# Sliding-window attention with a cosine-gated dense layer on one core: dense slots of two 256-token chunks in 512-column matmuls, a half-angle gate under a checked bound, late attention in two banks

## The chip, the cores and the metric

The kernel runs on one core of one Trainium2 chip. The metric is the device time of one execution in microseconds (us). The kernel before takes 733.99 us, the median of three runs (732.23 to 734.21).

## The reference

q, k and v have the shape (4 batches, 8 heads, 768 positions, 64). Attention keeps the first four positions (the sinks) and a window of 128 before each query. The dense layer has 3072 tokens, a model width of 512 and a hidden width of 2048, and its weights come as fp64.

```python
keep   = (pos[None, :] < n_sink) | ((rel >= 0) & (rel < window))     # rel = pos[:, None] - pos[None, :]
scores = where(keep, q @ k.T / sqrt(64), -1e9)
a      = exp(scores - max);  a = a / (sum(a) + 1e-9)
x      = (a @ v).transpose(0, 2, 1, 3).reshape(3072, 512)
h      = x @ w_in                # 512 -> 2048
g      = h * cos(h)
out    = g @ w_out               # 2048 -> 512
```

## The kernel before, in words

All large products run on PE as three fp32r matmuls, high by high, high by low and low by high, after each operand has been split into a high part (a rounding copy, on ACT) and a low part (a subtraction, on DVE).

The 3072 tokens are 12 chunks of 256 tokens (two query blocks of one batch). A chunk first goes through attention head by head. The heads of three of the four chunks that start a batch (24 heads) are "early": natural loads, turned on PE with transposes (L734), scores and values in plain fp32 matmuls (L771, L989), and the split of the result with a PE matmul that subtracts the high part (L340). The other 72 heads are "late": turned by DVE, split, scores L827 into bank `s`; the probabilities are turned on PE (L937) into bank `tp`, from where L960 (ACT) and L965 (DVE) read them; values L1013 go to bank `av`, read by L1020 (ACT) and L1027 (DVE). The sink columns of four heads at a time are turned on PE (L921), into bank `av` too.

Then the chunk goes through 8 dense slots, 96 slots in all. A slot takes two tiles of 128 hidden columns for the chunk's 256 tokens: 24 matmuls of 256 columns into one PSUM bank h (L391), whole turns of the angle on ACT (L400) and their removal on DVE (L406), the cosine on ACT (L413), the product h times cosine on DVE (L418), the high part of g on ACT (L424) and its low part on DVE or POOL (L430), and 12 matmuls of 512 columns (L439) that add into the chunk's two accumulator banks b0 and b1. Three banks take turns for h from the third chunk on. `xhi` and `xlo`, the split tokens, have two buffers each, so the next chunk's are written while this chunk's are read.

The weights are loaded as raw fp64 in pieces of 512 columns. Four bit operations and one subtraction turn a piece into fp32 and its two parts (L499, L505, L511, L535 on DVE, L532 on ACT). 32 pieces do this in the first sixth of the run, and later a DVE instruction a piece (L550) looks for weights that are too small for this. 120 fill matmuls (L1281), which compute nothing that is used, stand between the first instructions of PE.

The order of the instructions on each engine is fixed when the kernel is built: a planner lists the steps by due times, which the table C of numbers sets, and gives each step that can run on two engines to one of them. Every engine runs its list in that order.

Of the kernel before, what the change touches and what calls it, by code (L numbers as in the profile page):

```python
# [9 lines left out]
F32 = mybir.dt.float32  # L10
# [6 lines left out]
P = 128  # L17
# [10 lines left out]
    "ALT": 3.247, "BLF": 0.145, "CK": 63.541, "DA": -2.188, "DH": -1.258, "DM": -0.843, "DQ": 1.633, "DS": -3.217,  # L28
    "DV": 4.887, "DX": 6.133, "FILL": 120, "CL": 6.506, "GHI": 2, "GLO": 2, "L": 1, "LAG": 4.747, "LEAD": 22.987,
    "NEH": 24, "NM": 1.13, "NW": 0.46, "NWF": 0.209, "PB": 5, "PEN": 11.444, "POOLF": 1.457, "POOLPEN": 2.675, "R": 2,  # L30
    "RAW": 2, "SAME": 0.151, "SEM": 0.193, "SPE": 0.272, "STEP": 6.281, "T": 6.493, "TH": 3.647, "WARM": 5,
    "WARM2": 0, "P0": 10.087, "A0": -0.05, "D0": 9.99, "G0": 1.871, "S0": 1.917, "ZV": 33.968, "LD": -14.202,
    "HOT": 7.314, "RL": 4.633, "K0": -93.629, "K2": 8.334, "WI": -21.701, "WO": 0.716, "WS": -2.103, "WS2": 2.887,
    "WT": 2, "XV": 2,
}
MIN_TOP = 1.125 * 2.0**-15
# [134 lines left out]
def attn_moe_kernel(ctx, tc, q, k, v, n_sink, window, w_in, w_out, out):  # L171
# [17 lines left out]
    NSLOT = NFT // FG  # L189
    WP = 2 * FG * P  # L190

    NEH = int(C["NEH"]) // 2 * 2
    NE = -(-NEH // H)
# [12 lines left out]
    v32s = [lp.tile([P, KB, D], F32, name=f"v32_{n}") for n in range(C["XV"])]  # L206
    xb = lp.tile([P, NT], F32, name="xb")
# [6 lines left out]
    yt = lp.tile([P, FG, NT], I32, name="yt")  # L214
    rc_i = yt[:, 0].rearrange("p (a c) -> p a c", a=2)
# [6 lines left out]
    neg3 = cp.tile([P, 3], F32, name="neg")  # L222
    neg, quarter = neg3[:, 0:2], neg3[:, 2:3]
    lims = cp.tile([1, 2, 2, 2], F32, name="lims")
    tiny = cp.tile([P, NC * NSLOT // 2 + NFT], F32, name="tiny")
    redo = cp.tile([1, 1], I32, name="redo")

    def setup():
# [10 lines left out]
        nc.gpsimd.memset(xb, 0.0)  # L239
        nc.vector.memset(ones, 1.0)  # L240
        nc.vector.memset(quarter, HALF_PI_DOWN)
        for raw, src in env.first:
            nc.scalar.dma_start(out=raw.rearrange("p n w -> p (n w)"), in_=src)
        nc.scalar.activation(out=tiny[:, 0:1], in_=quarter, func=AF.Exp)
        nc.vector.memset(lims, 0.0)
# [44 lines left out]

    whi_in = wp.tile([P, NC, DFF], F32R, name="whi_in")
# [32 lines left out]
    def new_chunk():  # L324
        x = Rec()
        x.acc, x.o, x.f, x.bo = {}, {}, {}, {}
        x.sums = [[] for _ in range(NP)]
        x.parts = []
        return x

    def x_hi(x, a, p):
        def fn(e):
            if p == 0:
                x.hi = xp.tile([P, NP, NT], F32R, name=f"xhi_{a}", tag="xhi", bufs=2)
            nc.scalar.copy(out=x.hi[:, p, :], in_=x.f[p])
        return fn

    def x_minus(x, p):
        def fn(e):
            nc.tensor.matmul(  # L340
                out=x.f[p], lhsT=minus, rhs=x.hi[:, p, :], start=False, stop=True, skip_group_check=True
            )
        return fn

    def x_lo(x, a, p, early):
        def fn(e):
            if p == 0:
                x.lo = xp.tile([P, NP, NT], F32R, name=f"xlo_{a}", tag="xlo", bufs=2)
            if early:
                copy(e, x.lo[:, p, :], x.f[p])  # L350
            else:
                e.tensor_tensor(out=x.lo[:, p, :], in0=x.f[p], in1=f32(x.hi)[:, p, :], op=ALU.subtract)
        return fn

    def split_x(plan, x, a, p, t, early=False):

        add, buf = plan.add, plan.buf
        if p == 0:
            x.bhi, x.blo = buf("xhi", 2), buf("xlo", 2)
        i = add(  # L360
# [1192 lines left out]
```

## Time and profile before

| | |
|---|---|
| median of three runs | 733.99 us |
| the profiled execution | 733.03 us, its span 731.3 us |
| mean granted PE clock in the span | 0.998 |
| PE busy | 715.8 us, 98% |
| DVE busy | 614.5 us, 84% |
| ACT busy | 541.2 us, 74% |
| POOL busy | 165.8 us, 23% |

PE's busy time holds the fill matmuls too, and the ends of matmuls are modelled, so work is better counted by the starts of consecutive matmuls than by their durations. DVE and ACT overlap consecutive instructions a little as well. The busy shares are averages over stages: in the first stage the weights are converted and the first heads run, in the middle attention and dense slots are mixed, and the last 65 us are dense slots alone.

### The profile page before, as it was taken

The numbers are of one execution on the slowest core, as the hardware profiler recorded it, in microseconds if no ns is written. First come the engines' busy times: TensorE is split into PE (matmuls) and PEld (weight loads), VectorE is DVE, ScalarE is ACT, GpSimd is POOL, SyncE is SP. The second block draws the span as 40 slices with busy tenths as digits, with TensorE's granted clock in tenths as the row PEclk, the third lists the DMA queues.
The fourth block names the chain that finished last, engine by engine and source line by source line (L and its number), as shares of the span: only waits on it lengthen the run. The fifth ranks groups of instructions, "written<-read, shape, count | busy, mean of one in ns | idle before, by whom it ended". The sixth has DMA issues, their size and how long they took to land.

```text
span 731.3 us, 15326 instructions
## 1 busy us (share of the span) xinstructions
PE 715.8 (98%) x4865; PEld 651.3 (89%) x4865; DVE 614.5 (84%) x1811; ACT 541.2 (74%) x1354; POOL 165.8 (23%) x256
## 2 busy tenths in 40 slices
PE   8999999999999999999999999999999999999996
PEld 8887889899999999989898898999988999999995
DVE  6889999878999999899989988888898888875431
ACT  3878885987778868768778687788888697774332
POOL 1010100002242232433433324323110232321000
PEclk9999999999999999999999999999999999999999
DMA  6766564331673555646365443223333132110000
GB/s 174 199 183 185 166 173 136 83 55 32 139 193 55 121 134 128 158 118 170 78 159 149 89 99 58 49 69 55 55 73 64 30 83 52 34 45 3 28 2 34
DMA packets 215519, 71.51 MB, mean 98 GB/s; under 512 B 204164, under 2 KB 204164, under 8 KB 215428
## 3 DMA queue, kind: packets, MB, share of 16 engines
q1 hardware_dynamic: 215136, 69.38, 39.7%
q10 hardware_dynamic: 292, 1.05, 0.4%
q8 instruction: 41, 0.67, 0.4%
q14 instruction: 50, 0.41, 0.2%
HBM read 64.09 MB, written 6.29 MB: 96 GB/s over the span
## 4 chain that ended last, share of the span: by engine, by line
PE 71%; DVE 14%; ACT 7%; DMA 5%; issue 2%; SPq 1%; DVEq 0%; ACTq 0%
PE acc L439 28%; PE h L391 27%; PE av L1013 5%; PE s L827 4%; PE tp L937 2%; ACT p L858 2%; DVE wt L505 2%; DVE wt L511 1%; DMA xk<-in_k_dram 1%; PE idle L1281 1%; DMA raw<-in_moe_w_in_dram 1%; DVE r L406 1%; DVE p L849 1%; DVE glo L430 1%; DVE wt L499 1%
## 5 line engine op out<-in xcount | busy, mean ns | idle before, releaser
L391 PE MATMUL h<-xhi,whi_in 128*128 128x256 f32 x768 | 226.2, 295 | 0.7 <-DVE r L418 0.5
L391 PE MATMUL h<-xlo,whi_in 128*128 128x256 f32 x768 | 216.5, 282 | 0.0
L391 PE MATMUL h<-xhi,wlo_in 128*128 128x256 f32 x768 | 216.2, 282 | 0.0
L439 PE MATMUL acc<-whi_out,ghi 128*128 128x512 f32 x384 | 154.0, 401 | 0.2 <-DVE raw L382 0.2
L391 PEld LDWEIGHTS h<-xhi,whi_in 128*128 128x128 f32 x768 | 145.3, 189 | 8.5 <-DVE r L418 1.1
L439 PE MATMUL acc<-wlo_out,ghi 128*128 128x512 f32 x384 | 151.4, 394 | 0.0
L391 PEld LDWEIGHTS h<-xhi,wlo_in 128*128 128x128 f32 x768 | 145.5, 189 | 6.0
L439 PE MATMUL acc<-whi_out,glo 128*128 128x512 f32 x384 | 150.4, 392 | 0.0
L391 PEld LDWEIGHTS h<-xlo,whi_in 128*128 128x128 f32 x768 | 145.0, 189 | 0.0
L972 POOL TENSOR_SCALAR_AFFINE_SELECT ph<-ph 128x512 fp32r<-128x512 f32 x128 | 91.3, 714 | 112.4 <-DVE ph L965 95.5
L413 ACT ACTIVATE r<-r,neg 128x512 f32<-128x512 f32 x96 | 69.3, 724 | 45.4 <-DVE r L406 44.8
L430 DVE TENSOR_TENSOR glo<-r,ghi 128x512 fp32r<-128x512 f32 x92 | 67.8, 737 | 24.2 <-ACT ghi L424 23.5
L439 PEld LDWEIGHTS acc<-whi_out,glo 128*128 128x128 f32 x384 | 72.2, 188 | 16.3
L858 ACT ACTIVATE p<-p,st 128x136 f32<-128x136 f32 (+1 forms) x192 | 79.8, 417 | 0.4
L418 DVE TENSOR_TENSOR r<-h,r 128x512 f32<-128x512 f32 x96 | 65.5, 683 | 14.9 <-ACT r L413 14.8
L439 PEld LDWEIGHTS acc<-whi_out,ghi 128*128 128x128 f32 x384 | 72.5, 189 | 5.3 <-DVE raw L382 0.4
L439 PEld LDWEIGHTS acc<-wlo_out,ghi 128*128 128x128 f32 x384 | 72.8, 190 | 4.7 <-DVE wlo_out L535 0.3
L400 ACT ACTIVATE yt<-h 128x512 int32<-128x512 f32 x96 | 57.0, 594 | 23.6 <-PE h L391 23.1
L849 DVE CUSTOM_DVE_ANT_0 p<-s,mk 128x136 f32<-128x136 f32 (+1 forms) x192 | 59.2, 309 | 11.1 <-PE s L827 4.2
L406 DVE SCALAR_TENSOR_TENSOR r<-h,yt 128x512 f32<-128x512 f32 x96 | 65.2, 679 | 3.5 <-ACT yt L400 2.5
L424 ACT CAST ghi<-r 128x512 fp32r<-128x512 f32 x96 | 59.0, 614 | 11.0 <-PE acc L439 10.5
L878 POOL TENSOR_SCALAR p<-p,st 128x136 f32<-128x136 f32 (+2 forms) x38 | 20.7, 554 | 185.8 <-DVE st L868 108.4
(131 smaller groups left out, 1320.9 us busy)
## 6 DMA issues: line engine op xcount, KB each, us to landing
raw<-in_moe_w_out_dram SPq DMA_DIRECT2D x32, 512.0 KB
raw<-in_moe_w_in_dram SPq DMA_DIRECT2D x30, 512.0 KB
xk<-in_k_dram SPq DMA_DIRECT2D x256, 48.0 KB
v<-in_v_dram SPq DMA_DIRECT2D x64, 96.0 KB
out_dram<-raw SPq DMA_DIRECT2D x24, 256.0 KB
xq<-in_q_dram SPq DMA_DIRECT2D x144, 32.0 KB
xq<-in_q_dram SPq DMA_DIRECT2D x24, 64.0 KB
xk<-in_k_dram SPq DMA_DIRECT2D x24, 64.0 KB
```

The costliest lines, as they stand in the source:

```text
L391: nc.tensor.matmul(out=o.h[:, t, :], lhsT=w[:, c, fs], rhs=xx[:, c, :], start=(c == 0 and n == 0), stop=(c == NC - 1 and n == 2),)
L400: nc.scalar.activation(out=yt, in_=o.h, func=AF.Copy, scale=INV2PI, bias=0.25)
L406: nc.vector.scalar_tensor_tensor(out=o.r, in0=o.h, scalar=INV2PI, in1=yt, op0=ALU.mult, op1=ALU.subtract)
L413: nc.scalar.activation(out=o.r, in_=o.r, func=AF.Sin, scale=TWOPI_DOWN, bias=quarter)
L418: nc.vector.tensor_tensor(out=o.r, in0=o.h, in1=o.r, op=ALU.mult)
L424: nc.scalar.copy(out=o.ghi, in_=o.r)
L430: e.tensor_tensor(out=o.glo, in0=o.r, in1=f32(o.ghi), op=ALU.subtract)
L439: nc.tensor.matmul(out=x.acc[j], lhsT=gg[:, t, j * P : (j + 1) * P], rhs=w[:, f, :], start=(f == 0 and n == 0), stop=(f == NFT - 1 and n = ...
L849: nc.vector.tensor_tensor_reduce(out=o.pj[j][:, :w], in0=o.s_ps[j][:, :w], in1=masks[min(o.i0 + j, 2)][:, :w], op0=ALU.add, op1=ALU.min, s ...
L858: nc.scalar.activation(out=o.pj[j][:, :w], in_=o.pj[j][:, :w], func=AF.Exp, bias=o.lead.st[:, 0, o.nth, j : j + 1], scale=-1.0, accum_out= ...
L972: nc.gpsimd.affine_select(out=ph[:, :, b, :], in_=f32(ph)[:, :, 1, :], pattern=[[0, 2 * CB], [(-1, 1)[b], P]], compare_op=(ALU.is_gt, ALU. ...
L1013: nc.tensor.matmul(out=dst, lhsT=lhs, rhs=rhs, start=(n == 0), stop=(n == len(seq) - 1), skip_group_check=True)
```

## The change: what it does

- **Dense pairs.** The 12 chunks become 6 pairs. A slot takes one tile of 128 hidden columns for the pair's 512 tokens: 12 matmuls of 512 columns (L477) in place of 24 of 256. There are 96 slots as before, and the 1152 matmuls of `out_pair` (L522) are as many and as large as those of L439. A pair has four accumulator banks (b0, b1, b3, av); h has two banks (b4, b2).
- **Half-angle gate.** cos h = 1 - 2 sin(h/2)^2. ACT takes the sine of h/2 straight from PSUM (L486), the square is taken on ACT (56 of 96) or DVE (40), DVE forms (square - 0.5) times h (L499), and the high and low parts of g follow (L507, L513). The factor -2 is put into the copy out of the accumulators (L534, L536). L400 and L406 are gone. The sine needs a bound on h/2, which is checked in the last pair from norms of v and of w_in's columns.
- **Late attention in two banks.** The scores keep bank `s`; one tile `tl` holds the turned probabilities in its first half and the values, or the turned sink columns, in its second.
- **Order.** All four chunks that start a batch come first, as early heads (32 in place of 24). `xhi` and `xlo` are one buffer each, 512 tokens wide. 60 fill matmuls in place of 120. The checks of weights run as two ACT instructions on each of 64 half pieces (L637, L640). The numbers in table C differ.

```diff
-    "DV": 4.887, "DX": 6.133, "FILL": 120, "CL": 6.506, "GHI": 2, "GLO": 2, "L": 1, "LAG": 4.747, "LEAD": 22.987,
+    "DV": 3.222, "DX": 4.931, "FILL": 60, "CV": 5.546, "CL": 8.197, "HO": 0.7, "SX": -5.709, "CR": 18.376,
...
-    chunks = [(b, 0) for b in range(NE)]
-    chunks += [(b, i0) for b in range(B) for i0 in range(0, NB, CB) if i0 or b >= NE]
+    chunks = [(b, 0) for b in range(B)] + [(b, i0) for b in range(B) for i0 in range(CB, NB, CB)]
...
+    xhi = xp.tile([P, NP, PT], F32R, name="xhi")
+    xlo = xp.tile([P, NP, PT], F32R, name="xlo")
...
+    def split_late(plan, y, p, t):
+        add = plan.add
+        cs = slice(0, PT)
+        i = add([("ACT", act(PT))], x_hi(y, p, cs), [k for x in y.xs for k in x.sums[p]] + [y.bx[p // 2]], t)
+        j = add(sub(PT), x_lo(y, p, cs, False), [i, y.bx[p // 2]], t + 0.3, port=True)
...
+    def h_pair(o, half):
+        def fn(e):
+            if half == 0:
+                o.h = env.ps.tile([P, PT], F32, name=f"h_{o.m}", tag=o.bank)
+            fs = slice(o.s * P, o.s * P + P)
+            for c in range(half * NC // 2, (half + 1) * NC // 2):
+                for n, (w, xx) in enumerate(((whi_in, xhi), (wlo_in, xhi), (whi_in, xlo))):
+                    nc.tensor.matmul(
+                        out=o.h, lhsT=w[:, c, fs], rhs=xx[:, c, :],
+                        start=(c == 0 and n == 0), stop=(c == NC - 1 and n == 2),
+                    )
+        return fn
+    def half_sine(o):
...
+            nc.scalar.activation(out=o.r, in_=o.h, func=AF.Sin, scale=0.5)
...
+    def gate_square(o):
...
+            nc.vector.scalar_tensor_tensor(
+                out=o.r, in0=o.r, scalar=0.5, in1=o.h, op0=ALU.subtract, op1=ALU.mult
+            )
...
     def check_piece(plan, prio, k, src):
...
-            nc.vector.tensor_tensor_reduce(
-                out=t32, in0=top, in1=top, op0=ALU.mult, op1=ALU.max, scale=-1.0, scalar=-3.0e38,
-                accum_out=tiny[:, k : k + 1],
+            nc.scalar.activation(out=top, in_=top, func=AF.Square)
+
+        def below_floor(e):
+            nc.scalar.activation(
+                out=top, in_=top, func=AF.Relu, scale=-1.0, bias=floor, accum_out=tiny[:, k : k + 1]
             )
...
+    def check_columns(plan, prio, n):
+        r, bt, bl = buf("wt", C["WT"]), buf("tpl", 1), buf("l", C["L"])
...
+                nc.scalar.activation(out=w[:, min(c, 1)], in_=f32(whi_in)[:, c, fs], func=AF.Square)
...
+            nc.tensor.matmul(out=env.cs, lhsT=one_r, rhs=total[0], start=True, stop=True)
...
+        def late_bank(n):
+
+            if env.tl is None:
+                env.tl = ps.tile([P, 2, NT], F32, name="tl", tag="tp")
+            return env.tl[:, n]
...
-                o.tp = ps.tile([P, 4 * P], F32, name=f"tp_{o.tag}", tag=o.tp_tag)
                 if o.comb:
+                    o.tp = late_bank(0)
...
-                o.av = ps.tile([P, NT], F32, name=f"av_{o.tag}", tag="av")
+                o.av = late_bank(1)
```

Three places show how the order moves. The first is PE, the start of the program, where the first dense slot begins. In these rows `qk` are turned q and k, `s` scores, `tp` turned probabilities and `av` values, each with the pair of heads in its name; `idle` is the fill. Before:

```order
L734 MATMUL qk_0_2_488<-ident,xk 128x128 x2
L943 MATMUL tp_0_4_511<-ident,p_0_4_340 128x128 x3
L340 MATMUL av_0_2_466<-xhi_420,gt 128x256
L1281 MATMUL idle<-gt 128x256
L943 MATMUL tp_0_5_521<-ident,p_0_5_362 128x128 x3
L1281 MATMUL idle<-gt 128x256 x4
L771 MATMUL s_0_0_1_536<-tk_0_0_471,early 128x256
L989 MATMUL av_0_4_539<-early,vpe 128x256
L989 MATMUL av_0_4_539<-early,vpe 128x128
L391 MATMUL h_546<-xhi_420,whi_in 128x256
```

And in the changed kernel, where the batch at hand is already the second one:

```order
L1162 MATMUL tp_0_4_705<-ident,p_0_4_608 128x128 x3
L355 MATMUL av_0_2_674<-xhi,gt 128x256
L1162 MATMUL tp_0_5_714<-ident,p_0_5_622 128x128 x3
L980 MATMUL s_0_0_0_722<-tk_0_0_718,early 128x128
L477 MATMUL h_726<-xhi,whi_in 128x512
L477 MATMUL h_726<-xhi,wlo_in 128x512
L477 MATMUL h_726<-xlo,whi_in 128x512
```

The first dense matmul stood behind the values of four heads of one batch, with fills between the rows; now it stands behind those of twelve heads of two batches, with no fill in sight.

The second place is PE in the middle of the run, with the semaphores that a row waits for: the turn of a head's probabilities, and the values of the head before it. Before, in two banks, `tp` and `av`:

```order
L827 MATMUL s_2_7_0_2310<-r_0_2_7_2290,l_2_7_2268 128x264 [waits DVE_49]
L937 MATMUL tp_2_3_2314<-ident,p_2_3_1919 128x128 [waits DVE_49]
L937 MATMUL tp_2_3_2314<-ident,p_2_3_1919 128x128
L439 MATMUL acc_1_1674<-whi_out,ghi_2094 128x512
L439 MATMUL acc_1_1674<-wlo_out,ghi_2094 128x512
L439 MATMUL acc_1_1674<-whi_out,glo_2115 128x512
```

And in the changed kernel, where L1231 writes the values and L1152 the turned probabilities into the two halves of `tl`:

```order
L1231 MATMUL tl<-ph_4_6_3299,vr_4_6_3296 64x256
L1231 MATMUL tl<-ph_4_6_3299,vr_4_6_3296 128x128
L1231 MATMUL tl<-ph_4_6_3299,vr_4_6_3296 64x128
L522 MATMUL acc_0_2199<-whi_out,ghi_3264 128x512
L522 MATMUL acc_0_2199<-wlo_out,ghi_3264 128x512
L522 MATMUL acc_0_2199<-whi_out,glo_3269 128x512
L1152 MATMUL tl<-ident,p_4_7_2966 128x128 [waits Activation_49]
L1152 MATMUL tl<-ident,p_4_7_2966 128x128
```

The turn waited for DVE, which makes the probabilities and reads the bank `tp`; now it waits for ACT, and three accumulator matmuls stand between it and the values whose readers use the other half of its bank.

The third place is PE where one set of tokens ends and the next begins. Before, `xhi_2306` is another buffer than that of the slots ahead of it:

```order
L439 MATMUL acc_0_2476<-whi_out,ghi_2872 128x512
L439 MATMUL acc_0_2476<-wlo_out,ghi_2872 128x512
L439 MATMUL acc_0_2476<-whi_out,glo_2887 128x512
L391 MATMUL h_2864<-xhi_2306,whi_in 128x256
L391 MATMUL h_2864<-xhi_2306,wlo_in 128x256
L391 MATMUL h_2864<-xlo_2342,whi_in 128x256
L391 MATMUL h_2864<-xhi_2306,whi_in 128x256 [waits Activation_49]
L391 MATMUL h_2864<-xhi_2306,wlo_in 128x256
L391 MATMUL h_2864<-xlo_2342,whi_in 128x256 [waits DVE_49]
```

And in the changed kernel, where the last matmul that reads the old `xhi` stands 18 matmuls ahead of the first that reads the new one:

```order
L522 MATMUL acc_2_2225<-whi_out,ghi_3342 128x512
L522 MATMUL acc_2_2225<-wlo_out,ghi_3342 128x512
L522 MATMUL acc_2_2225<-whi_out,glo_3348 128x512
L477 MATMUL h_3470<-xhi,whi_in 128x512 [waits Activation_49]
L477 MATMUL h_3470<-xhi,wlo_in 128x512
L477 MATMUL h_3470<-xlo,whi_in 128x512 [waits DVE_49]
L477 MATMUL h_3470<-xhi,whi_in 128x512 [waits Activation_49]
L477 MATMUL h_3470<-xhi,wlo_in 128x512
L477 MATMUL h_3470<-xlo,whi_in 128x512 [waits DVE_49]
```

With one buffer, the writes of the new `xhi` (ACT) and `xlo` (DVE) have moved into the gap between these two matmuls.

## Rows read from the trace of the kernel before

**Rows 1.** The page's first part: busy us, share, instructions.
```profile
PE 715.8 (98%) x4865; PEld 651.3 (89%) x4865; DVE 614.5 (84%) x1811; ACT 541.2 (74%) x1354; POOL 165.8 (23%) x256
```
**Rows 2.** Windows by stage: length, busy us by engine, PE clock, DMA share, GB/s.
```profile
36.50:103.10 66.60, 62.83 (x421) 55.48 (x421) 62.03 (x157) 56.27 (x143) 7.39 (x10) 1.00 0.62 178
103.10:160.10 57.00, 56.84 (x369) 51.60 (x370) 51.99 (x136) 44.12 (x102) 2.59 (x3) 1.00 0.40 101
160.10:660.00 499.90, 497.52 (x3468) 455.93 (x3467) 445.03 (x1374) 394.36 (x998) 150.27 (x225) 1.00 0.41 92
```
**Rows 3.** PE timeline: the first dense matmul; columns start us, us.
```profile
36.46 0.37 PE L391 MATMUL h<-xhi,whi_in 128*128 128x256 f32 x1
```
**Rows 4.** PE timeline of the dense stretch, two cycles of 6 and 3 matmuls.
```profile
690.41 0.28 PE L391 MATMUL h<-xhi,whi_in 128*128 128x256 f32 x1
...
691.12 0.40 PE L439 MATMUL acc<-whi_out,ghi 128*128 128x512 f32 x1
...
691.82 0.28 PE L391 MATMUL h<-xhi,whi_in 128*128 128x256 f32 x1
...
693.94 0.40 PE L439 MATMUL acc<-whi_out,ghi 128*128 128x512 f32 x1
...
694.63 0.28 PE L391 MATMUL h<-xhi,whi_in 128*128 128x256 f32 x1
```
**Rows 5.** Groups by line and shape: busy us, mean ns, idle before.
```profile
L391 PE MATMUL h<-xhi,whi_in 128*128 128x256 f32 x768 | 226.2, 295 | 0.7 <-DVE r L418 0.5
L406 DVE SCALAR_TENSOR_TENSOR r<-h,yt 128x512 f32<-128x512 f32 x96 | 65.2, 679 | 3.5 <-ACT yt L400 2.5
L424 ACT CAST ghi<-r 128x512 fp32r<-128x512 f32 x96 | 59.0, 614 | 11.0 <-PE acc L439 10.5
L400 ACT ACTIVATE yt<-h 128x512 int32<-128x512 f32 x96 | 57.0, 594 | 23.6 <-PE h L391 23.1
L1027 DVE TENSOR_TENSOR x<-av,xb 64x256 f32<-64x256 f32 x72 | 29.7, 412 | 6.0 <-ACT xb L1020 4.7
L1020 ACT COPY xb<-av 64x256 f32<-64x256 f32 x72 | 26.7, 370 | 23.7 <-PE av L1013 22.4
L878 DVE TENSOR_SCALAR p<-p,st 128x136 f32<-128x136 f32 x64 | 15.3, 297 | 0.1
L499 DVE TENSOR_SCALAR wt<-raw 128x512 int32<-128x512 int32 x32 | 13.4, 420 | 3.0 <-DMA raw<-in_moe_w_in_dram 1.7 <-DMA raw<-in_moe_w_out_dram 1.3
```
**Rows 6.** DVE timeline: two instructions back to back.
```profile
68.58 0.68 DVE L535 TENSOR_TENSOR wlo_out<-wt,whi_out 128x512 fp32r<-128x512 f32 x1
69.18 0.68 DVE L430 TENSOR_TENSOR glo<-r,ghi 128x512 fp32r<-128x512 f32 x1
```
**Rows 7.** PE timeline: the turns, scores and values of an early head.
```profile
28.67 0.38 PE L734 MATMUL qk<-ident,xk 128*128 128x128 f32 x2
28.89 0.39 PE L771 MATMUL s<-tk,early 128*128 128x128 f32 x2
29.03 0.60 PE L1281 MATMUL idle<-gt 128*128 128x256 f32 x3
29.47 0.65 PE L771 MATMUL s<-tk,early 128*128 128x256 f32 x2
29.96 0.82 PE L989 MATMUL av<-early,vpe 128*128 128x256 f32 x4
```
**Rows 8.** Waits of PE by line: total us, times, longest.
```profile
PE tp L937 <- DVE ph L965: 0.8, 1, 0.8
```
**Rows 9.** All engines' timeline: PE's last matmul and the copy behind it.
```profile
724.99 0.39 PE L439 MATMUL acc<-whi_out,glo 128*128 128x512 f32 x1
725.42 0.59 ACT L380 COPY raw<-acc 128x512 f32<-128x512 f32 x1 [0.77 <-PE acc L439]
```
**Rows 10.** Windows of one us after PE's last matmul, columns as in rows 2.
```profile
727.00:728.00 1.00, 0.00 (x0) 0.00 (x0) 0.00 (x0) 0.00 (x0) 0.00 (x0) 0.91 0.67 231
728.00:729.00 1.00, 0.00 (x0) 0.00 (x0) 0.00 (x0) 0.00 (x0) 0.00 (x0) 0.50 0.02 6
```

More of the change, by code (lines that the diff above doesn't have):

```diff
@@ L327, in new_chunk, with new_pair, x_hi @@
         x.sums = [[] for _ in range(NP)]
-        x.parts = []
         return x
-    def x_hi(x, a, p):
+    def new_pair(d, xs):
+        y = Rec()
+        y.d, y.xs = d, xs
+        y.acc, y.o, y.bo = {}, {}, {}
+        y.parts = [[] for _ in range(NP)]
+        for n, x in enumerate(xs):
+            x.n, x.y = n, y
+        return y
+    def x_hi(y, p, cs):
         def fn(e):
-            if p == 0:
-                x.hi = xp.tile([P, NP, NT], F32R, name=f"xhi_{a}", tag="xhi", bufs=2)
-            nc.scalar.copy(out=x.hi[:, p, :], in_=x.f[p])
+            nc.scalar.copy(out=xhi[:, p, cs], in_=y.f(p, cs))
@@ new lines, in g_hi_pair, with fn, g_lo_pair, out_pair @@
+    def g_hi_pair(o):
+        def fn(e):
+            o.ghi = mp.tile([P, PT], F32R, name=f"ghi_{o.m}", tag="ghi", bufs=C["GHI"])
+            nc.scalar.copy(out=o.ghi, in_=o.r)
+        return fn
+    def g_lo_pair(o):
+        def fn(e):
+            o.glo = mp.tile([P, PT], F32R, name=f"glo_{o.m}", tag="glo", bufs=C["GLO"])
+            e.tensor_tensor(out=o.glo, in0=o.r, in1=f32(o.ghi), op=ALU.subtract)
+        return fn
+    def out_pair(o, y, j):
+        def fn(e):
+            f = o.s
+            if f == 0:
+                y.acc[j] = env.ps.tile([P, DM], F32, name=f"acc_{o.m}_{j}", tag=y.banks[j])
+            for n, (gg, w) in enumerate(((o.ghi, whi_out), (o.ghi, wlo_out), (o.glo, whi_out))):
+                nc.tensor.matmul(
+                    out=y.acc[j], lhsT=gg[:, j * P : (j + 1) * P], rhs=w[:, f, :],
+                    start=(f == 0 and n == 0), stop=(f == NFT - 1 and n == 2),
+                )
+        return fn
@@ L1341, in banded_path @@
                 waiting = []
[L1342 to L1355 removed]
+        dense_slots(len(ys) - 1)
@@ new lines, in banded_path, with most_of @@
+        most = cp.tile([P, NV + 1], F32, name="most")
+        row = cp.tile([P, 1], F32, name="row")
+        end = cp.tile([1, 8], F32, name="end")
+        def most_of(e):
+            nc.vector.tensor_reduce(
+                out=most[:, :NV], in_=vsum.rearrange("p (n k) -> p n k", k=NB), axis=mybir.AxisListType.X, op=ALU.max
+            )
+            if checks:
+                nc.vector.tensor_reduce(out=most[:, NV:], in_=tiny, axis=mybir.AxisListType.X, op=ALU.max)
+            else:
+                nc.vector.memset(most[:, NV:], -3.0e38)
@@ L1369, in again, with most_turn, most_row, row_turn @@
+        def most_turn(e):
+            env.tp = env.tl[: NV + 1, 0, :P]
+            nc.tensor.transpose(out=env.tp, in_=most, identity=ident)
+        def most_row(e):
+            nc.vector.tensor_reduce(out=row[: NV + 1], in_=env.tp, axis=mybir.AxisListType.X, op=ALU.max)
+        def row_turn(e):
+            env.tp = env.tl[:1, 0, : NV + 1]
+            nc.tensor.transpose(out=env.tp, in_=row[: NV + 1], identity=ident[: NV + 1, : NV + 1])
         def again(e):
             limits()
-            if not checks:
-                nc.vector.tensor_copy(out=redo, in_=flag)
-                return
```

488 lines of the change are left out of this document (335 added, 153 removed), and 6 rows, old and new, of the table C.

## The prediction

> **What bounds the kernel now.** I read the busy shares first, then the same by stage, then PE's timeline and waits. PE is busy 715.8 of 731.3 us, DVE 614.5 and ACT 541.2 [rows 1]. The stages differ. From 160 us to 660 us PE is busy 497.5 of 499.9 us, DVE 445.0, ACT 394.4 [rows 2]: PE bounds alone, and DVE has 11% of slack. From the first dense matmul at 36.46 us [rows 3] to 103 us DVE is busy 62.0 of 66.6 us (93%) and PE only 62.8, so there the conversion of weights on DVE sets the pace, and before 36 us fills stand between PE's rows (one is in [rows 7]). After 103 us PE is full again. So three things can change the time: the length of PE's own list, the DVE-bound first 100 us, and new waits in a stretch in which PE has hardly one: the longest between a turn of probabilities and a reader of its bank is a single 0.8 us [rows 8].
>
> **PE's list.** Six h matmuls of 256 columns take 0.71 us (690.41 to 691.12), three accumulator matmuls of 512 columns 0.70 (691.12 to 691.82) or 0.69 (693.94 to 694.63) [rows 4]. Two of 256 are thus 0.71/3 = 0.2367 us and one of 512 is 0.695/3 = 0.2317: merging saves 5.0 ns. The 2304 become 1152, so 1152 x 5.0 ns = -5.8 us; with the rounding of a row's 0.01 us, -3.8 to -7.7. The accumulator matmuls stay as they are.
>
> The page "TensorE: Matmul & The Clock Gate" of the Trainium skill (section "Back-to-back issue gap") gives an isolated matmul N/2.4 + 2.5 ns, by which merging would save one 2.5 ns each, 2.9 us in all, and a sustained 131 ns for 512 columns with weight loads, at which the saving would be of another size altogether. The rows show 232 ns in a sustained stream, so the second figure does not hold here, and the first is near but low; the row decides.
>
> Eight heads turn from late to early. Of an early head, PE does two turns of q or k in 0.22 us (28.67 to 28.89), two score matmuls in 0.14 (28.89 to 29.03) and two in 0.49 (29.47 to 29.96) [rows 7], 0.85 us. A late head has no such turns, and four score matmuls of up to 264 columns at an h matmul's spacing, 0.118 us of 256 [rows 4], some 0.48. The values are alike to a tenth. That is 0.4 to 0.5 us a head; I take 0.5, 8 x 0.5 = +4.0 us (bounds 2.4, and 6.8 if late scores were free). Eight one-row matmuls of the column check, at most 0.118 us each: +0.9. Four fewer subtracting matmuls L340: -0.5. The list: -5.8 + 4.0 + 0.9 - 0.5 = **-1.4 us**. The 60 fills less (60 x 0.118 = 7.1 us) I cost at nothing: they fill time in which PE has to wait for DVE anyway. If they did stand in the way, it would be a gain of up to 7 us.
>
> **The start.** Counting the instructions ahead of the first dense matmul, DVE has 98 before and 162 after: twelve heads are done there, not four. At the 0.22 us each of the sum below those 64 are 14 us, so I expect the first dense matmul near 50 us, not 36. That alone is no loss, since the heads are done earlier by as much. What counts is DVE's list up to the same amount of PE work. Up to some 90 us of it (before: the 11th dense slot), DVE has 296 instructions before and 333 after, of which dense 25 and 15, weights 118 and 94 (six of the 24 are L499's), and others 153 and 224, mostly the scaling of probabilities and copies out of PSUM. One instruction of 512 columns costs 0.60 us from start to start (68.58 to 69.18, though each lasts 0.68 [rows 6]), so 0.08 comes off every duration: L499 0.42 - 0.08 = 0.34, L878, standing for the others, 0.30 - 0.08 = 0.22 [rows 5]. The sum: -10 x 0.60 - 18 x 0.60 - 6 x 0.34 + 71 x 0.22 = -3.2 us. At DVE's 93% that is 3.4 us of time. ACT comes out about equal at that place: the turns L400 (57.0 us over the whole run [rows 5]) are gone, the squares and more copies are new. I take a little more, **-5 us**, because a list with fewer weights is less apt to wait for DMA: the bound is 7% of 66.6, 4.7 us more, so -8 below; above, +3, if the new order waits more often, as before's 36 us at first do.
>
> **The middle.** L406 (65.2 us of DVE) and L400 leave; a square (ACT or DVE), and the checks on ACT in the later pairs, come. DVE and ACT lists remain shorter than PE's in every stage after 103 us, so none of this counts unless PE waits. Two places may make it wait.
>
> At the end of a pair `xhi` is a single buffer. Between the last matmul that reads the old and the first that reads the new stand nine accumulator matmuls (9 x 0.232 = 2.1 us) and attention's nine (some 1 us), 3.1 us. In it ACT must cast two pieces (0.61 each [rows 5]) and DVE subtract two (0.68), some 1.9 us in a chain, and they have the slot's own sine, square and cast to do as well, up to 2 us more. Each of five ends costs 0 to 1.5 us; I take 0.3. With as much for waits on the two h banks (before three), **+2 us** (0 to +8).
>
> The other place is `tl`, the rival below; in the sum it stands at nothing, since three accumulator matmuls (0.70 us) cover one read of 0.37.
>
> **The end.** The last matmul starts at 724.99 and the copy behind it, 0.59 us, at 725.42 [rows 9]. Halved over two engines it saves 0.2 us. The final checks sit ahead of it and are over by then.
>
> **The sum.** The profiled execution took 733.03 us: 733.03 - 1.4 - 5 + 2 - 0.2 = 728.4. The median of the runs is 0.96 above it, so **729.4 us**.
>
> **Rivals.**
>
> *Two halves of one bank.* In the order, turns of a head wait for the reader of the other half, which they had no need of in two banks. The values' readers are L1020, 0.37 us on ACT, then L1027, 0.41 on DVE [rows 5]. ACT is busy 79% of the time [rows 2] with instructions of some 0.6 us; a reader that comes on a busy engine waits 0.3 us on average, 0.24 over all, then takes 0.37, and the result of the matmul before it is some 0.16 late (0.28 lasts, 0.12 spacing [rows 4]): 0.77 against 0.70 of cover. So the mean is on the edge, and some waits last half a microsecond. At 0.25 us for each of the 64 late heads that is +16 us: 728.4 + 16 + 0.96 = **745.4 us**, slower. It decides from 0.11 us a head (6.8 us, up to 736.2) on; the bound, both reads uncovered for each head, is 64 x 0.78 = 50 us. For it: the order lists such waits about 21 times within one reader's length. Against it: PE before also waits for banks in nearly every head, and nearly none shows.
>
> The page "PSUM — Partial Sum Buffer" of the Trainium skill (sections "Terms" and "PSUM bank collisions raise a hardware error") says that two engines may not touch one bank in the same partitions at once, even at different addresses, so the halves cannot be used side by side. No row of before shows two halves of a bank in use; the waits in the order agree with the rule.
>
> *No gain at the start.* PE's -1.4 and the end's -0.2 stay, the start gives nothing because what DVE saves is spent on waits of the new order, and the middle costs 2: 733.03 + 0.4 + 0.96 = **734.4 us**, no change. For it: DVE has 37 more instructions in that stretch, and the first dense slot comes later.
>
> *A larger gain at the start.* DVE and ACT no longer wait there, and fewer fills let PE follow at once: -12 in place of -5, and no waits in the middle: 733.03 - 1.4 - 12 - 0.2 + 0.96 = **720.4 us**. For it: 98 of the fills stand ahead of the first dense matmul in the order (98 x 0.118 = 11.6 us), and PE is idle 3.8 us between 36 and 103 us [rows 2]: 15 us that no term has touched. Against it: the list of DVE, which sets the pace there, gets only 3.2 us shorter.
>
> *The clock.* With 60 fewer fills PE may idle at the start, and after PE's last matmul the granted clock goes to 0.91 within some two us and then 0.50 [rows 10]. A stretch at 0.50 in the first 50 us would double matmuls there, but under a DVE that sets the pace; +5 us is the price I see: **734 us**, with no change.
>
> **How the numbers follow.** A measurement of this kernel can tell 0.3% from no change, 2.2 us: below 731.8 is faster, above 736.2 slower. The forecast (724 to 731.8) has 0.40, the larger gain 0.12, no gain at the start with the clock 0.20, the bank's two halves 0.18, and longer waits at the ends of pairs (up to +8, 737) 0.10. So faster 0.52, same 0.20, slower 0.28. The range reaches from 718, under the larger gain, to 746, the rival of the bank.
>
> **What would show it.** In the changed profile: consecutive h matmuls 0.232 us apart (else the first term fails); the first dense matmul near 50 us, and the end of the first pair earlier than before's same amount of PE work, with DVE above 93% in that stretch; PE's idle time after 110 us under 6 us, and in the list of waits `tl` behind ACT or DVE under 3 us in all. If `tl` has 10 us there, the rival of the bank is right. Waits of h for `xhi` at five places show the price of the single buffer. The forecast is wrong if PE idles longer after 110 us than before, or if the first 110 us are not shorter for the same work.

## The result, and the profile after

The changed kernel takes 737.15 us, the median of five runs (736.53 to 738.47), the kernel before beside it 733.99 us (731.65 to 734.66). The ratio is 1.0054, with a 95% interval from 1.0032 to 1.0076: **slower by half a per cent, some 4 us, where 729.4 us, a gain of 4.6 us, was forecast**. The profiled execution has a span of 736.8 us.

The first part of the page of the changed kernel (busy us, share, instructions; against [rows 1]):

```profile
PE 711.8 (97%) x3674; PEld 582.2 (79%) x3674; DVE 591.0 (80%) x1757; ACT 564.4 (77%) x1486; POOL 150.1 (20%) x229
```

PE has 1191 matmuls less and is busy 4 us less, yet the span is 5.5 us longer: PE stands idle 25.0 us (736.8 - 711.8) where it stood idle 15.5. The windows say where (length, then busy us of PE, PEld, DVE, ACT and POOL, PE clock, DMA share, GB/s). Before, then after:

```profile
0.00:80.00 80.00, 73.11 (x471) 64.82 (x471) 68.24 (x202) 58.32 (x164) 8.53 (x22) 1.00 0.65 183
80.00:660.00 580.00, 577.27 (x3997) 528.38 (x3996) 519.16 (x1563) 458.48 (x1147) 154.68 (x230) 1.00 0.42 96
```

```profile
0.00:80.00 80.00, 72.26 (x408) 59.46 (x409) 69.78 (x238) 60.41 (x182) 6.20 (x18) 1.00 0.65 171
80.00:660.00 580.00, 571.06 (x2966) 468.12 (x2965) 485.33 (x1446) 468.02 (x1236) 143.87 (x211) 1.00 0.44 102
49.70:118.00 68.30, 65.59 (x329) 51.66 (x329) 61.59 (x170) 55.11 (x140) 2.79 (x4) 1.00 0.58 161
```

Up to 80 us PE is busy about as long, with half the fills: without them (120 and 60 times 0.118 us) 58.9 us before and 65.2 after, or 61.1 and 65.6 if the fills' modelled durations are taken out instead. The two are not the same work, since twelve heads and not four are now done ahead of the first dense matmul. From 80 to 660 us it stood idle 2.7 us before and 8.9 now, though DVE is busy 34 us less. The first dense matmul starts at 49.74 us (36.46 in [rows 3]), and DVE is busy 90% of the stretch behind it (third line).

In the dense stretch near the end (PE's timeline, start and duration in us; against [rows 4]) six h matmuls of 512 columns take 1.36 us (691.59 to 692.95) and three accumulator matmuls 0.68 (690.91 to 691.59), 0.227 us each:

```profile
690.91 0.39 PE L522 MATMUL acc<-whi_out,ghi 128*128 128x512 f32 x1
...
691.59 0.39 PE L477 MATMUL h<-xhi,whi_in 128*128 128x512 f32 x1
...
692.95 0.39 PE L522 MATMUL acc<-whi_out,ghi 128*128 128x512 f32 x1
```

The groups that stand for those of [rows 5] (busy us, mean ns, idle before):

```profile
L499 DVE SCALAR_TENSOR_TENSOR r<-r,h 128x512 f32<-128x512 f32 x96 | 65.3, 681 | 13.5 <-ACT r L492 12.8
L486 ACT ACTIVATE r<-h 128x512 f32<-128x512 f32 x96 | 57.0, 595 | 35.5 <-PE h L477 35.1
L492 ACT ACTIVATE r<-r 128x512 f32<-128x512 f32 x56 | 35.2, 630 | 0.6
L494 DVE TENSOR_TENSOR r<-r 128x512 f32<-128x512 f32 x40 | 29.2, 729 | 3.3 <-ACT r L486 2.7
L1183 DVE TENSOR_TENSOR ph<-tl,ph 128x256 fp32r<-128x256 f32 x64 | 26.6, 416 | 1.4 <-ACT ph L1178 0.8 <-PE tl L1136 0.2
L1178 ACT CAST ph<-tl 128x256 fp32r<-128x256 f32 x64 | 23.7, 371 | 5.4 <-DVE raw L1250 3.7 <-PE tl L1152 0.7
```

The new operations cost about what others of this width do: the sine from PSUM 0.60 us, the square 0.63 on ACT and 0.73 on DVE. The list of PE's waits (total us, times, longest; against [rows 8]) is headed by what is new:

```profile
PE tl L1136 <- DVE ph L1183: 5.4, 9, 1.0
```

L1136 turns the sink columns of four heads into the second half of `tl`; L1183 reads the turned probabilities of a head from the first half. No wait of h for `xhi` or `xlo` is in the list. One of the nine, in the timeline of all engines:

```profile
350.42 0.38 PE L1152 MATMUL tl<-ident,p 128*128 128x128 f32 x2
...
351.85 0.35 ACT L1178 CAST ph<-tl 128x256 fp32r<-128x256 f32 x1
...
352.28 0.40 DVE L1118 CAST gc<-p 128x16 fp32r<-128x16 f32 x4
352.49 0.39 PE L522 MATMUL acc<-whi_out,glo 128*128 128x512 f32 x1
352.59 0.42 DVE L1120 TENSOR_TENSOR gc<-p,gc 128x16 f32<-128x16 f32 x4
352.94 0.41 DVE L1183 TENSOR_TENSOR ph<-tl,ph 128x256 fp32r<-128x256 f32 x1
353.40 0.43 PE L1136 MATMUL tl<-ident,gc 128*112 128x128 f32 x2 [0.53 <-DVE ph L1183]
```

The turn of the probabilities starts at 350.42. Its reader on ACT comes 1.4 us later, behind other work. On DVE the eight small instructions that make the sink columns (L1118, L1120) stand ahead of the second reader, L1183. The columns are ready at 353.01, but the sink turn waits until L1183 has left the other half, at 353.35.

### The profile page after: what moved, and what is told of

Read it like the earlier page. It is cut to its first block, busy times and chain, and to the rows that moved or that the text cites. A ratio compares the mean times of both kernels' runs of the same rounds, so it can differ in the third digit from the quotient of the medians.

```text
span 736.8 us, 13122 instructions
## 1 busy us (share of the span) xinstructions
PE 711.8 (97%) x3674; PEld 582.2 (79%) x3674; DVE 591.0 (80%) x1757; ACT 564.4 (77%) x1486; POOL 150.1 (20%) x229
## 5 line engine op out<-in xcount | busy, mean ns | idle before, releaser
L522 PE MATMUL acc<-whi_out,ghi 128*128 128x512 f32 x384 | 159.5, 415 | 0.0
L477 PE MATMUL h<-xhi,whi_in 128*128 128x512 f32 x384 | 154.3, 402 | 0.0
L522 PE MATMUL acc<-whi_out,glo 128*128 128x512 f32 x384 | 150.8, 393 | 0.0
L522 PE MATMUL acc<-wlo_out,ghi 128*128 128x512 f32 x384 | 150.5, 392 | 0.0
L477 PE MATMUL h<-xlo,whi_in 128*128 128x512 f32 x384 | 150.4, 392 | 0.0
L477 PE MATMUL h<-xhi,wlo_in 128*128 128x512 f32 x384 | 150.1, 391 | 0.0
L513 DVE TENSOR_TENSOR glo<-r,ghi 128x512 fp32r<-128x512 f32 x96 | 69.4, 723 | 33.5 <-ACT ghi L507 33.4
L507 ACT CAST ghi<-r 128x512 fp32r<-128x512 f32 x96 | 59.1, 616 | 43.2 <-PE acc L522 37.8
L522 PEld LDWEIGHTS acc<-whi_out,glo 128*128 128x128 f32 x384 | 72.1, 188 | 16.3
L477 PEld LDWEIGHTS h<-xlo,whi_in 128*128 128x128 f32 x384 | 72.1, 188 | 16.2
L486 ACT ACTIVATE r<-h 128x512 f32<-128x512 f32 x96 | 57.0, 595 | 35.5 <-PE h L477 35.1
L477 PEld LDWEIGHTS h<-xhi,whi_in 128*128 128x128 f32 x384 | 72.3, 188 | 13.8 <-DVE r L499 0.2
L477 PEld LDWEIGHTS h<-xhi,wlo_in 128*128 128x128 f32 x384 | 72.3, 188 | 13.2
L522 PEld LDWEIGHTS acc<-whi_out,ghi 128*128 128x128 f32 x384 | 72.5, 189 | 8.8
L522 PEld LDWEIGHTS acc<-wlo_out,ghi 128*128 128x128 f32 x384 | 72.6, 189 | 7.9
L499 DVE SCALAR_TENSOR_TENSOR r<-r,h 128x512 f32<-128x512 f32 x96 | 65.3, 681 | 13.5 <-ACT r L492 12.8
L1036 PE MATMUL s<-r,l 128*128 128x264 f32 x256 | 54.9, 294 | 0.5
L1036 PEld LDWEIGHTS s<-r,l 128*128 128x128 f32 x256 | 45.8, 188 | 11.9 <-issue 2.7
L1044 DVE COPY_PREDICATED s<-mk,s 128x128 f32<-128x128 int32 x128 | 36.7, 287 | 17.6 <-PE s L1036 16.9
```

Source lines behind the costliest of these rows:

```text
L477: nc.tensor.matmul(out=o.h, lhsT=w[:, c, fs], rhs=xx[:, c, :], start=(c == 0 and n == 0), stop=(c == NC - 1 and n == 2),)
L486: nc.scalar.activation(out=o.r, in_=o.h, func=AF.Sin, scale=0.5)
L499: nc.vector.scalar_tensor_tensor(out=o.r, in0=o.r, scalar=0.5, in1=o.h, op0=ALU.subtract, op1=ALU.mult)
L507: nc.scalar.copy(out=o.ghi, in_=o.r)
L513: e.tensor_tensor(out=o.glo, in0=o.r, in1=f32(o.ghi), op=ALU.subtract)
L522: nc.tensor.matmul(out=y.acc[j], lhsT=gg[:, j * P : (j + 1) * P], rhs=w[:, f, :], start=(f == 0 and n == 0), stop=(f == NFT - 1 and n == 2),)
```

## The experiments

Theory A: late attention's two halves of one bank make PE wait. Rival B: the waits come from the rest of the change (two h banks, single token buffers, DVE and ACT being late), or the gains forecast are not there. Each ratio is to the kernel before, run on the same chip.

**Two late banks, e2_banks.** The fourth accumulator shares the third one's bank, and the bank it leaves takes the second half of `tl`. The two accumulators are summed into one, so these rows of the output are not the product's.

```diff
-            y.bacc = [buf(b, 1) for b in banks]
+            y.bacc = [buf(b, 1) for b in banks[:3]]
+            y.bacc.append(y.bacc[2])
...
+            if n and env.tl1 is None:
+                env.tl1 = ps.tile([P, 2, NT], F32, name="tl1", tag="av")
+            return (env.tl, env.tl1)[n][:, n]
```

> The changed kernel with its two halves of tl in two banks of their own (the turned probabilities in one, the values and sink columns in the other). The bank for it is taken from the fourth accumulator, whose products are added into the third one's bank, so those rows of the output are not the reference's; the work of every engine stays the same. Theory A, the shared bank makes PE wait: the waits of the sink turn for a reader of the other half (5.4 us of idle time in nine waits) go, and with the shorter ones behind accumulator matmuls 7 to 10 us; 727 to 730. Rival B, the waits in the middle come from the two h banks, the single token buffers or ACT and DVE being late by themselves: 735 to 738, and the same idle time turns up at other lines.

729.26 us, ratio 0.9944 (0.9926 to 0.9962): 1.1% or 8.1 us below the changed kernel. The window and the waits of PE:

```profile
80.00:660.00 580.00, 576.34 (x3015) 479.00 (x3014) 493.40 (x1454) 482.06 (x1265) 147.09 (x220) 1.00 0.46 105
```

```profile
PE tl L1140 <- DVE gc L1122: 2.7, 4, 0.7
```

PE idles 3.7 us from 80 to 660 us in place of 8.9; what is left of the sink turn's wait is for the columns themselves. That is theory A.

One thing besides the banks changed in e2_banks, and "the work of every engine stays the same" does not hold for it: its planner also saw other buffers, and from 305 us on the engines' lists differ (DVE has 1743 instructions in place of 1757, POOL 238 in place of 229). Up to there all four lists are the same, so the first late head's turn and the 19th's, in the changed kernel and then in e2_banks, compare the banks alone:

```profile
185.15 0.38 PE L1152 MATMUL tl<-ident,p 128*128 128x128 f32 x2
...
305.18 0.38 PE L1152 MATMUL tl<-ident,p 128*128 128x128 f32 x2
```

```profile
183.62 0.38 PE L1156 MATMUL tl<-ident,p 128*128 128x128 f32 x2
...
300.84 0.38 PE L1156 MATMUL tl<-ident,p 128*128 128x128 f32 x2
```

The lead of e2_banks grows from 1.53 to 4.34 us, 2.8 us in 18 heads or 0.16 us a head; over all 64 it grows to 10.09 us (625.19 against 615.10), 0.14 us a head. So the moved lists are not what made it faster. The spans of these two profiles, 736.8 and 725.0 us, lie further apart than the medians do, so their rates are a little high.

729.26 is also close to the forecast of 729.4, made without a price for `tl`. That agreement is in part luck, since some terms of the sum were not measured by themselves and others were off (see why the prediction was wrong).

**The shared bank alone, e3_before32 and b32_tl.** First the kernel before with 32 early heads, then the same with the late heads' two banks made one tile.

```diff
-    "NEH": 24
+    "NEH": 32
```

```diff
-                o.av = ps.tile([P, NT], F32, name=f"av_{o.tag}", tag="av")
+                o.av = env.tl[:, 1]
...
+                    o.tp = env.tl[:, 0]
```

> The kernel before with 32 early heads instead of 24 (the same constant of its table; all four chunks that start a batch come first), nothing else changed. Theory A, eight early heads cost what the traces' spacing gives, 6 us of PE, rather than the 4.0 of the prediction: 739 to 742, with the last h matmul of the run later by as much. Rival B, they cost 4 us or less: 734 to 738. The order was not tuned for it, so a few us more at the start would belong to neither; the PE idle time in the first 120 us tells them apart.

> The kernel before with 32 early heads (745.6 us, 1.0162 of before, already run) and, new here, turned probabilities and values or sink columns of its 64 late heads in two halves of one tile tl, as in the changed kernel; every list in the same order, its third h bank and its accumulators as they are. Theory A, the shared bank alone costs what the run with two banks gave back, 8 us: 751 to 756, ratio near 1.027, with waits of PE for the other half's readers. Rival B, it costs only together with the pairs (four accumulators, two h banks, slots of 512): within 2 us of 745.6.

745.63 us, ratio 1.0162 (1.0143 to 1.0181), and with one tile 751.71 us, 1.0238 (1.0222 to 1.0254): the bank alone, with every list in the same order, costs 0.76%, 5.6 us. That is theory A at the low end of its 751 to 756, and far from B's 2. The first of the two missed its range, 739 to 742: eight more early heads took 12 us in a list of instructions that was not tuned for them, and this run does not say how much of it is the heads. PE's waits in e3_before32, then in b32_tl:

```profile
PE s L827 <- DVE st L849: 2.3, 4, 1.0
PE h L391 <- DVE r L418: 1.7, 2, 1.3
```

```profile
PE h L392 <- DVE r L419: 2.5, 5, 1.3
PE s L828 <- DVE st L850: 1.7, 3, 1.0
...
PE tl L940 <- ACT gt L381: 1.1, 5, 0.2
PE tl L940 <- DVE p L879: 0.7, 1, 0.7
```

Here the price is not in one long wait at one place but in many short ones, of `h` as well as of `tl`: the span grew by 5.1 us (744.8 to 749.9) and PE's idle time by only 2.5 (from 744.8 - 724.4 to 749.9 - 727.0), since a wait shorter than a matmul's modelled end counts as busy.

**Moving the waiting instruction, a_sink1, e5b_sinktp and e5_onebuf.** a_sink1 puts each of the 16 sink turns one dense step later on PE; e5b_sinktp puts the sink turn into the other half of `tl`; e5_onebuf tells the planner that the two halves are one buffer.

```diff
+        steps = move_sinks(steps, 1)          # a_sink1
...
-                o.gp = late_bank(1)[:GR]
+                o.gp = late_bank(0)[:GR]       # e5b_sinktp
...
-            bav = buf("avl" if o.comb else o.av_tag, 1)
+            bav = buf("tpl" if o.comb else o.av_tag, 1)   # e5_onebuf
```

> The changed kernel with the 16 sink turns on PE each moved behind the next dense step of PE's list (three accumulator or six h matmuls), nothing else moved on any engine. In the trace a sink turn waits for DVE's reader of the other half of tl, which stands behind the eight instructions that make the sink columns. Theory A, that wait is what the shared bank costs most: its 5.4 us and the hidden part go, 3 to 6 us less than the changed kernel, 731 to 734. Rival B, the wait moves to the values behind the sink turn or to the next turn: 736 to 738.

> The changed kernel with the turned sink columns in the half of tl that the turned probabilities use, under that half's buffer in the planner's books, instead of in the half of the values. Theory A, the sink turn is where the shared bank costs most, since nothing in the plan puts it behind the readers of the probabilities' half: its 5.4 us of waits go, the smaller waits of the other turns stay, the time falls by 4 to 6 us, to 731 to 733. Rival B, the waits are spread over all turns: less than 2 us, 735.5 to 737.5.

> The changed kernel with the planner told that the two halves of tl are one bank: turned probabilities, sink columns and values of the late heads take turns in one buffer of its books instead of in two, so that the list of PE has each of them behind the last reader of the one before; the instructions are the same, some 560 of PE's stand elsewhere. Theory A, the price of the shared bank (8 us by the run with two banks) is that of an order made without knowing of it: PE's waits for the other half go or are filled with dense matmuls, and the time falls by 4 to 8 us, to 729 to 733. Rival B, the bank itself is too slow for the heads in any order, a chain of some 3 us a head: the waits move to other rows of attention, time 736 to 745.

All three were slower than the changed kernel, and none came out in a range of either theory: 744.65 us, ratio 1.0164 (1.0143 to 1.0185); 743.25 us, 1.0133 (1.0111 to 1.0155); 787.3 us, 1.0718 (1.0691 to 1.0745). In a_sink1, where nothing else was moved, the waits moved to the next instructions and grew; its waits and its window:

```profile
PE tl L1176 <- DVE ph L1207: 5.2, 8, 1.0
PE tl L1255 <- ACT ghi L528: 2.1, 2, 1.1
```

```profile
80.00:660.00 580.00, 566.75 (x2936) 462.48 (x2935) 477.77 (x1438) 461.80 (x1221) 144.90 (x211) 1.00 0.44 101
```

L1176 there is the turn of the next head's probabilities, L1255 the values. PE idles 13.3 us in place of 8.9: the wait went where rival B said, but the time rose by some 8 us (1.0164 against 1.0054), which neither theory had: the turns and values behind the sink turn wait more than the sink turn did. So another place of the sink turn does not take the wait away. e5b_sinktp decides nothing: the sink turn's wait for the other half is gone from its list, but the planner made other lists for all engines, and PE waits 3.4 us ahead of scores and 3.3 ahead of h instead. In e5_onebuf, where the halves are taken strictly in turns, PE's waits and two windows are:

```profile
PE tl L1231 <- POOL ph L1190: 9.4, 5, 2.4
PE h L477 <- DVE r L499: 7.9, 5, 3.0
PE s L1036 <- DVE st L1058: 5.6, 6, 1.8
```

```profile
300.00:320.00 20.00, 12.96 (x52) 9.68 (x53) 14.73 (x54) 14.80 (x44) 4.01 (x9) 0.66 0.43 110
320.00:404.00 84.00, 84.00 (x446) 70.30 (x445) 64.36 (x193) 69.93 (x191) 26.95 (x42) 1.00 0.41 90
```

PE is full for long stretches and then stands idle in bunches; in the one shown PE stood idle a third of the time, first from 298.18 to 300.01, and the granted clock has a mean of 0.66, so it was at 1.2 and not at 2.4 GHz for most of it. Over the span the clock is 0.961 (0.997 in the changed kernel), which by itself may be up to 28 us of the 50 (an estimate: 788.1 x 0.039 less 736.8 x 0.003). So the 50 us are not the price of the bank alone. The run shows that this planner makes a worse list when its books have one buffer; whether another order could hide the bank is not shown.

**The merged matmul, e4_h256.** Each h matmul of 512 columns as two of 256.

```diff
+                    for hs in (slice(0, NT), slice(NT, PT)):
+                        nc.tensor.matmul(
+                            out=o.h[:, hs], lhsT=w[:, c, fs], rhs=xx[:, c, hs],
```

> The changed kernel with each h matmul of 512 columns issued as two of 256 over the two chunks, in the same order and the same banks; the lists of the other engines are word for word the same. Theory A, merging saves only the 5.0 ns a pair that the dense stretch showed: 737 + 5.8 = 743. Rival B, it saves what h matmuls took in all, 285.1 us before against 269.6 after from start to start, since those of 256 columns also run late wherever attention stands between them: 737 + 15 = 750 to 753.

743.67 us, ratio 1.0136 (1.0117 to 1.0156): 0.82% or 6.0 us above the changed kernel. That is theory A; the forecast's term was 5.8. In its dense stretch six pairs of 256 columns take 1.43 us and three accumulator matmuls 0.70 again:

```profile
694.19 0.40 PE L478 MATMUL h<-xhi,whi_in 128*128 128x256 f32 x2
...
695.62 0.40 PE L524 MATMUL acc<-whi_out,ghi 128*128 128x512 f32 x1
...
696.32 0.40 PE L478 MATMUL h<-xhi,whi_in 128*128 128x256 f32 x2
```

**The fills, e6_fill120, a_dblfill, a_halffill, b_halffill.** 120 in the changed kernel's table; then, with all other instructions in their places, each of its 60 twice, and every second one left out; and every second of the 120 of the kernel before left out.

```diff
-    "FILL": 60
+    "FILL": 120        # e6_fill120
...
         def fill(n):
             def fn(e):
+                if n % 2:
+                    return     # a_halffill, b_halffill
```

> The changed kernel with 120 fill matmuls as before, in place of 60. Theory A, fills stand where PE waits for DVE and ACT anyway: within 1.5 us of 737. Rival B, the start's gain of 5.8 us over the kernel before is the 60 fills that are gone (60 x 0.118 = 7.1 us): 742 to 744. Rival C, PE's clock profits from them: below 735.

> The changed kernel with each of its 60 fill matmuls issued twice in its place, 120 in all, and every list otherwise word for word the same (with 120 set in the table the lists had moved too). Theory A, fills stand where PE waits anyway: within 1 us of 737. Rival B, they stand on the path: up to 60 x 0.118 = 7 us more, 741 to 744, as the table's 120 gave 741.7.

> The changed kernel with every second of its 60 fill matmuls left out, 30 in all, every list otherwise word for word the same. Theory A: within 1 us of 737, since what is left covers waits for DVE and DMA. Rival B, fills still stand on the path: 733.5 to 736 (at most 30 x 0.118 = 3.5 us). Rival C, the clock falls in the first 50 us: above 738.

> The kernel before with every second fill matmul left out, 60 instead of 120, and every list otherwise word for word the same. Theory A, the fills hid nothing and cost nothing: within 1 us of 733.5. Rival B, part of the changed kernel's earlier start is its 60 fewer fills, and the kernel before gains it too: 728 to 732. Rival C, PE's clock needs them: slower than 735, with a granted clock below 0.99.

e6_fill120 741.73 us, ratio 1.0117 (1.0096 to 1.0137); a_dblfill 742.01, 1.0122 (1.01 to 1.0145); a_halffill 738.01, 1.0065 (1.0046 to 1.0084); b_halffill 732.31, 0.9995 (0.9983 to 1.0007). In the changed kernel 60 fills more cost 4.6 to 5.0 us, 30 fewer give nothing; in the kernel before 60 fewer give nothing. That fits fills that are free up to what PE has to wait anyway. The price of nothing in the prediction holds if the 60 are taken from the kernel before; put back on top of the rest of the change, they cost up to 5 us. That the fewer fills alone made the earlier start (rival B of b_halffill) falls.

**DVE's relief, e8_glo2, b_half and b_half_fill.** The low part of g computed twice in the changed kernel; the half-angle gate alone in the kernel before, and the same with half the fills. In the last two the check of the bound is left out.

```diff
+            for _ in range(2):
                 e.tensor_tensor(out=o.glo, in0=o.r, in1=f32(o.ghi), op=ALU.subtract)
```

```diff
-            nc.scalar.activation(out=yt, in_=o.h, func=AF.Copy, scale=INV2PI, bias=0.25)
...
-            nc.scalar.activation(out=o.r, in_=o.r, func=AF.Sin, scale=TWOPI_DOWN, bias=quarter)
+            nc.scalar.activation(out=o.r, in_=o.h, func=AF.Sin, scale=0.5)
+            nc.scalar.activation(out=o.r, in_=o.r, func=AF.Square)
```

> The changed kernel with the low part of g computed twice, one write over the other, 96 more DVE instructions of 0.72 us (69 us, about what the half-angle gate took off DVE: 65 us of L406), all orders otherwise the same. Theory A, DVE's relief is worth nothing in the middle, where PE bounds, and only its share of the start counts, some 9 of the slots at 0.6 us: 737 to 744, nearly all of it in the first 120 us. Rival B, the shorter chain of the gate is what the two h banks live on: 750 or more, with PE waiting for glo and h all along.

> The kernel before with the half-angle gate alone: the turns L400 and their removal L406 give no instruction, the cosine L413 becomes the sine of h/2 from PSUM and a square, both on ACT, the product L418 becomes (square - 0.5) times h, the factor -2 is in the copy out; every list otherwise the same. The check of the bound on h/2 is left out. DVE does 65 us less, ACT about the same. Theory A, PE bounds after 100 us, and DVE's relief counts only in the start, where nine slots have 0.6 us less each: 728 to 731. Rival B, DVE's relief is worth half of itself everywhere, as twice the low part of g cost 33 us of 69 in the changed kernel: 700 to 715 cannot be, since PE's list is 686 us, but 722 to 727. Rival C, ACT's chain is longer, since sine and square stand where the cosine stood: 734 or more.

> The kernel before with the half-angle gate alone and every second fill matmul left out; the check of the bound on h/2 is left out. By themselves the gate gave 0.9985 of before and the fills 0.9995. Theory A, in the start DVE and ACT set the pace together, and with the gate's relief the fills begin to stand in the way, so that the two add up to more than each: 728 to 731. Rival B, neither bounds anything: 732 to 734.

e8_glo2: 770.26 us, ratio 1.0499 (1.0474 to 1.0523), 33 us more for 69 us of DVE. Its page and waits of PE:

```profile
PE 725.6 (94%) x3674; PEld 582.4 (76%) x3674; DVE 663.1 (86%) x1853; ACT 566.0 (74%) x1486; POOL 159.5 (21%) x229
```

```profile
PE s L1037 <- DVE st L1059: 8.1, 11, 1.6
PE tl L1137 <- DVE ph L1184: 4.8, 10, 1.1
PE s L1037 <- DVE r L1028: 2.7, 13, 0.5
```

DVE is at 86% and PE waits for it, mostly for attention's parts and not for the gate's chain. That is rival B in its size, but not in its mechanism. b_half: 733.08 us, ratio 0.9985 (0.9973 to 0.9997), 1.1 us less for 50 us less of DVE (614.5 to 564.5), between the ranges of A (to 731) and C (from 734): next to nothing. b_half_fill: 731.19 us, ratio 0.9975 (0.9962 to 0.9987); the two add up within the noise (0.9980 would be the sum), between the ranges of A and B. Of the kernels that compute the whole output it is the fastest, 1.8 us below the one before, but without the check.

**The end, e1_whole.** The last accumulator is copied out whole.

```diff
-            whole = not last or j < NJ - 1
+            whole = True
```

> The changed kernel with the very last accumulator copied out whole by one engine, as the other copies are, instead of in two halves on ACT and DVE. Theory A, the split costs time at the end: in the changed kernel DVE's half starts 0.43 us after its matmul's end and the span ends 7.8 us after PE's last matmul, against 5.9 us before; unsplit, the end should come back to about 6.0 us and the time fall by 1.5 to 1.9 us, to about 735.5. Rival B, the end is longer because of the three stores that stand behind one another whatever their size: the time stays within 0.5 us of 737.

737.7 us, ratio 1.0055 (1.0039 to 1.007), as the changed kernel. In the changed kernel's profile the end, from the last matmul's end, is 7.8 us long: the last matmul starts at 728.60, ACT's half follows in the pair of copies from 728.35, DVE's half only at 729.45, when ACT's is done (its bracket names ACT), and three stores are issued until 732.06 (against [rows 9]):

```profile
728.35 1.06 ACT L534 ACTIVATE raw<-acc 128x512 f32<-128x512 f32 x2
...
728.60 0.39 PE L522 MATMUL acc<-whi_out,glo 128*128 128x512 f32 x1
728.97 3.09 SPq L543 DMA_DIRECT2D out_dram<-raw  x3
729.45 0.42 DVE L536 TENSOR_SCALAR raw<-acc 128x256 f32<-128x256 f32 x1 [4.73 <-ACT raw L534]
```

So the two halves, which lie in one bank, were copied one after the other, and the split gave nothing. In e1_whole's profile the end is 6.2 us, but its time shows no gain. One profile does not settle it: in the runs that left the end as it was it is 6.4 us (e5b_sinktp) to 7.8 (e4_h256) long. By the time this is rival B; the two intervals together allow 2 us, and it stays open.

## Why the prediction was wrong, point by point

- **The step that failed** is the end of the part on the middle: "in the sum it stands at nothing, since three accumulator matmuls (0.70 us) cover one read of 0.37". `tl` costs 8.1 us in the changed kernel (e2_banks) and 5.6 in a kernel whose lists did not change at all (b32_tl); 5.2 us of the 8.1 are time that PE idles more from 80 to 660 us, the rest would be in waits too short to show as idle, as in b32_tl. The working had the length of a read and left out the queue ahead of the reader. In the timeline above the turn's readers end 2.9 us after it, 1.4 of it until ACT comes to it, and 0.7 more until DVE has made the sink columns. Six h and three accumulator matmuls were not enough cover. The prediction's own sign said so too: after 110 us PE idles 16.9 us, 8.3 before (the ends included).
- The rival for this had the mechanism and a size, 0.25 us a head; measured, 8.1 / 64 = 0.13 us, just above the 0.11 from which it was to decide. Its sign, 10 us of `tl` in the list of waits, did not come, since the list has only the 5.4 us that show. It had a chance of 0.18, with "PE before also waits for banks in nearly every head, and nearly none shows" against it. That was read off a kernel that had two banks, so it said nothing on one. b32_tl shows that the bank costs most of it (5.6 us) without the pairs too.
- **Merging** came out at 6.0 when undone, 5.8 forecast, but the reason given is only half right. The h matmuls are 0.227 us apart, not 0.232, and so are the accumulators' (below). By the dense stretch the saving would be 1152 x (0.2367 - 0.227) = 11 us and some 5 more on the accumulators. Of these 16 only 6.0 show in the time, so the agreement is luck in part; why no more show is open.
- **The start**: the first dense matmul came at 49.74 us ("near 50"), and the count without fills has PE 4.5 to 6.3 us ahead at 80 us, against 5 forecast, though not with the same work. But DVE is at 90%, not "above 93%", and the parts tried in the kernel before (gate 1.1, fills 0.4 us) give 1.8 together; the rest would have to come from the order, and no run shows that by itself.
- **The eight early heads** were not measured cleanly: e3_before32 took 12 us. That the time without `tl` is 729.3 allows the 4.0, but one term may hide another: the start, these heads and the two h banks were never taken apart.
- **"None of this counts unless PE waits"**, of DVE's relief: right for the kernel before, where 50 us less of DVE gave 1.1 us (b_half). In the changed one as much DVE work put back costs half of itself (e8_glo2), so there the relief does count: DVE is 84% busy from 80 to 660 us and has slack on average, but too little where attention hands over.
- **Ends of pairs**: no wait of h for the single buffers shows; 0.3 us each was enough. **The clock** stayed at 1.00 in the changed kernel.
- **The end of the program** is 6.4 to 7.8 us long, 5.9 before, where -0.2 was forecast: the halves were copied in turn, not side by side. What the split costs in time stays open (e1_whole).

## What to carry to other kernels

Two halves of one bank were waited for here as one buffer, whether by PE that writes or by ACT and DVE that read; no run tried to use both at once. Price such sharing by the time from the write until the last reader has left, the queues ahead of the readers included, and not by the readers' own length. A low wait in a profile is evidence only for the buffers that it was taken with. And a run that takes just one term out tells whether that term was wrong, but a sum that then agrees does not vouch for each of the others.

## What the runs showed that was not expected

The accumulator matmuls, the same in both kernels, became faster by their neighbours: in the dense stretch three take 0.70 or 0.69 us beside h matmuls of 256 columns [rows 4] and 0.68 beside those of 512 (above); in e4_h256, with 256 columns again, they are back at 0.70. And moving 32 of 3674 matmuls by one step cost some 8 us (a_sink1, 1.0164 against 1.0054): in an order this tight a small move by hand can cost as much as the bank itself.
